# Sparse attention with two MLP layers on one core: scores made once with queries on partitions, the masked weights transposed by TensorE, and late conversion of three quarters of the last weights

## Chip, core and metric

The kernel runs on one core of a Trainium2 chip. The core has five engines that run their own instruction streams and meet at semaphores: PE (TensorE, matrix products, with its weight loads shown apart as PEld), DVE (VectorE), ACT (ScalarE), POOL (GpSimd) and SP (SyncE), which here only issues transfers. The metric is the device time of one execution in microseconds (us); lower is better. Matmuls read SBUF and write PSUM, which has eight banks of 2 KB per partition.

## What is computed

```python
def _attn_ref(q, k, v, tau):                      # 4 batches, 8 heads, 576 tokens, 64 wide
    scores = scale * np.matmul(q, k.transpose(0, 1, 3, 2))
    thresh = np.max(scores, axis=-1, keepdims=True) - tau
    scores = np.where(scores >= thresh, scores, -1000000000.0)
    scores = scores - np.max(scores, axis=-1, keepdims=True)
    attn = np.exp(scores)
    attn = attn / (np.sum(attn, axis=-1, keepdims=True) + 1e-09)
    return np.matmul(attn, v)

def _moe_ref(x, w_in, w_out, g_ln):               # 2304 x 512 -> 1024 -> 512
    h = x @ w_in
    e = np.exp(h - np.max(h, axis=-1, keepdims=True))
    solu = h * e / (np.sum(e, axis=-1, keepdims=True) + 1e-09)
    mu = np.mean(solu, axis=-1, keepdims=True)
    var = np.mean((solu - mu) ** 2, axis=-1, keepdims=True)
    return ((solu - mu) / np.sqrt(var + 1e-06) * g_ln) @ w_out

def _moe2_ref(x, w_in, w_out):                    # 2304 x 512 -> 2048 -> 512
    h = x @ w_in
    return (h * np.tanh(softplus(h))) @ w_out
```

The attention keeps only keys whose score lies within tau of the row's largest one. The four weight matrices arrive as 64-bit floats and are turned into 32-bit ones on the device.

## The kernel before

**Planner.** Every instruction is a task with an engine, a duration, its data and buffer dependencies (`Plan.add`, line 65). `Plan.run` (line 198) tries a list scheduler with several weights and emits the shortest order that it found. The order on each engine is fixed by that: an instruction that waits holds everything behind it on its engine. Buffers are named slots with a number of turns (`buf(pool, tag, shape, dtype, turns)`).

**Attention, heads n = 0 to 31.** `operands` (line 480) loads K and Q of a head with the 64 dimensions twice on the 128 partitions, and makes a rounded high half and a residue of each, so that two one-pass matmuls (high Q, low Q against stacked K) give an accurate product. Then the scores are made twice:

- `s_tile` (line 502), five tiles of 128 queries (the fifth is half empty): queries on partitions, four matmuls of 288 columns into a PSUM tile `st`, then one DVE maximum over the 576 keys (line 517). `m_chain` (line 523) turns the five maxima of a head into thresholds, rounds and transposes them (six lines of small DVE work, 526 to 532), and sends them by a transfer (line 534) into two extra rows of the operand `Qb`.
- `unit` (line 538), five units: keys on partitions this time, four more matmuls of 288 columns (line 548), which subtract the threshold by the two extra rows. ACT copies the scores out of PSUM to `xu` (line 559), ACT takes the exponential (line 560), DVE masks (line 561). One unit in five handles the half key tile and goes from PSUM directly (lines 555 and 561).

`pv` (line 579) multiplies V with the masked weights, which already have keys on partitions. In heads 0 to 15 (`n < SB0`) these are plain 32-bit matmuls (two instructions each, line 597); in heads 16 to 31 weights and V are split into halves (ACT line 566, DVE or POOL line 574) and take three one-pass matmuls. The half key tile always goes through a split (line 566, POOL line 568, matmuls 607 and 608). ACT moves the result and the row sums out of the single bank `acc` (lines 619 and 620), and `norm` divides.

**First MLP, token tiles 0 to 17** (4.5 per batch): `x_split`, `moe_h` (line 663, 24 matmuls of 512 columns into a two-bank tile `mo`), `layer_norm`, `moe_t` (line 704, eight 128x128 PE transposes, line 716, into `mo`), `moe_y` (line 730, matmuls of 256 columns). A tile needs the whole attention of its batch, so this MLP of one batch runs beside the attention of the next.

**Second MLP** (line 787 on): the hidden width is cut into four groups q = 0 to 3, and the tokens into nine pieces p of 256. `ff_in` and `ff_out` run 96 matmuls of 256 columns per group and piece, and pieces go in pairs with 512 columns after the first six. Group q uses one of two weight buffers (`b_w`), so that group q+2 waits for group q. Pool changes order the stages: `o_a` when the operands of attention are free, `o_b` after the attention, `o_c` after the first MLP; groups 1 and 3 wait for `o_c`.

**Weights.** `convert` (line 383) loads a 128x256 piece of 64-bit numbers and needs two ACT, three DVE and one POOL instruction (line 404). There are 96 pieces: 32 of the first MLP, 64 of the second. The 64 are stored to a scratch in memory (`store`, line 416); `split_w2` (line 842) loads them back later and splits them into halves (lines 857 and 861).

## Time and profile before

| | |
|---|---|
| median of three runs | 1069.92 us (1067.49 to 1074.01) |
| the profiled execution | 1072.17 us |
| its span, first to last instruction | 1070.4 us |
| PE busy | 979.0 us (91%), 5696 matmul instructions |
| DVE, ACT, POOL busy | 670.5, 711.6, 438.5 us |
| mean granted clock of PE | 0.97 of full speed |
| memory traffic of the span | 117 GB/s |

A busy PE is not a PE at its peak: the time of one matmul instruction in the profile includes its way through the pipeline, so that the times of consecutive ones overlap. The steady cost of one is read from the distance between starts. The profile's stretches therefore have to be read with two numbers for PE, the busy time and the work (instructions times steady cost). A row of a stretch gives the engines in the order PE, PEld, DVE, ACT, POOL.

### The profile page before, as it was taken

The numbers are of one execution on the slowest core, as the hardware profiler recorded it, in microseconds if no ns is written. First come the engines' busy times: TensorE is split into PE (matmuls) and PEld (weight loads), VectorE is DVE, ScalarE is ACT, GpSimd is POOL, SyncE is SP. The second block draws the span as 40 slices with busy tenths as digits, with TensorE's granted clock in tenths as the row PEclk, the third lists the DMA queues.
The fourth block names the chain that finished last, engine by engine and source line by source line (L and its number), as shares of the span: only waits on it lengthen the run. The fifth ranks groups of instructions, "written<-read, shape, count | busy, mean of one in ns | idle before, by whom it ended". The sixth has DMA issues, their size and how long they took to land.

```text
span 1070.4 us, 16653 instructions
## 1 busy us (share of the span) xinstructions
PE 979.0 (91%) x5696; PEld 860.3 (80%) x5696; DVE 670.5 (63%) x1416; ACT 711.6 (66%) x1312; POOL 438.5 (41%) x434
## 2 busy tenths in 40 slices
PE   5886889798699988988988999999999999999998
PEld 4765677677599878877988998998888888888887
DVE  7888888888888878777687646433245434322222
ACT  4977778888687778787798867655577467521220
POOL 5665666466655745655636332222022412300000
PEclk8988899899799999998999999999999999999999
DMA  6333333233222222231213863489665566422311
GB/s 184 100 102 84 92 92 93 69 94 102 73 79 78 73 80 66 55 94 53 56 37 97 255 206 108 129 262 366 199 216 187 182 197 207 153 79 99 118 50 70
DMA packets 109849, 132.03 MB, mean 123 GB/s; under 512 B 18634, under 2 KB 80010, under 8 KB 109764
## 3 DMA queue, kind: packets, MB, share of 16 engines
q1 hardware_dynamic: 109620, 130.96, 39.6%
q8 instruction: 45, 0.74, 0.3%
q14 instruction: 40, 0.33, 0.1%
q10 hardware_dynamic: 144, 0.00, 0.0%
HBM read 99.68 MB, written 25.69 MB: 117 GB/s over the span
## 4 chain that ended last, share of the span: by engine, by line
PE 61%; ACT 6%; DVE 4%; issue 1%; POOL 0%; DMA 0%; ACTq 0%; POOLq 0%
PE o L918 13%; PE h L892 12%; PE smt L739 8%; PE mo L671 7%; PE h2b L892 6%; PE o2b L918 5%; PE acc L597 3%; PE st L548 2%; PE st L513 2%; ACT hi L566 1%; ACT e L560 1%; ACT xu L559 1%; PE mo L716 1%; DVE so L689 1%; DVE e L561 1%
## 5 line engine op out<-in xcount | busy, mean ns | idle before, releaser
L404 POOL TENSOR_TENSOR cf<-cf,cl 128x256 uint32<-128x256 uint32 x96 | 78.9, 826 | 207.7 <-DVE cf L402 148.1
L517 DVE TENSOR_REDUCE m<-st 128x1 f32<-128x576 f32 x160 | 119.1, 748 | 54.3 <-PE st L513 53.3
L561 DVE SCALAR_TENSOR_TENSOR e<-xu,thr,e 128x576 f32<-128x576 f32 x128 | 115.2, 906 | 3.8 <-ACT e L560 3.3
L597 PE MATMUL acc<-e,V 128*128 128x288 f32 x256 | 81.7, 450 | 24.4 <-DVE e L561 17.4
L560 ACT ACTIVATE e<-xu,sc 128x576 f32<-128x576 f32 x128 | 98.7, 773 | 6.2 <-POOL lo L574 3.5
L513 PE MATMUL st<-Kst,Qhh 128*128 128x288 f32 x320 | 78.7, 329 | 18.3 <-DVE Kst L490 7.3
L559 ACT ACTIVATE xu<-st 128x576 f32<-128x576 f32 x110 | 70.9, 645 | 30.8 <-DVE e L561 15.8
L739 PE MATMUL smt<-LH,W2H 128*128 128x256 f32 x288 | 82.1, 285 | 0.4 <-DVE yl L750 0.3
L739 PE MATMUL smt<-LL,W2H 128*128 128x256 f32 x288 | 81.7, 284 | 0.0
L739 PE MATMUL smt<-LH,W2L 128*128 128x256 f32 x288 | 81.7, 284 | 0.0
L597 PEld LDWEIGHTS acc<-e,V 128*128 128x128 f32 x256 | 48.7, 206 | 40.9 <-DVE e L561 11.1
L574 POOL TENSOR_TENSOR lo<-e,hi 128x576 fp32r<-128x576 f32 x32 | 48.1, 1505 | 79.4 <-ACT hi L566 54.8
L513 PEld LDWEIGHTS st<-Kst,Qhh 128*128 128x128 f32 x320 | 54.9, 201 | 28.6 <-ACT xu L559 8.1
L597 PE MATMUL acc<-hi,V 128*128 128x288 f32 x256 | 64.6, 310 | 10.2 <-ACT ss L620 9.4
L548 PE MATMUL st<-Qhh,Kst 128*128 128x288 f32 x274 | 67.4, 328 | 6.7 <-DVE er L561 2.5
L513 PE MATMUL st<-Kst,Qb 128*128 128x288 f32 x320 | 71.6, 307 | 0.0
L942 DVE TENSOR_TENSOR acc<-acc,o 128x512 f32<-128x512 f32 x36 | 24.8, 688 | 69.8 <-PE o L918 69.8
L345 ACT ACT_TABLE_LOAD x52 | 66.7, 1283 | 1.6 <-PEq L987 0.7
L548 PE MATMUL st<-Qb,Kb 128*128 128x288 f32 x274 | 60.9, 304 | 5.3 <-DMA Qb<-mr 5.3
L490 POOL TENSOR_TENSOR Kst<-K,Kst 64x640 fp32r<-64x640 f32 x31 | 51.6, 1665 | 27.5 <-ACT Kst L489 16.6
L548 PEld LDWEIGHTS st<-Qhh,Kst 128*128 128x128 f32 x274 | 47.4, 198 | 15.3 <-ACT xu L559 4.8
L568 POOL TENSOR_TENSOR ph<-er,ph 64x576 fp32r<-64x576 f32 x32 | 46.7, 1459 | 29.4 <-ACT ph L566 19.8
(180 smaller groups left out, 3149.5 us busy)
## 6 DMA issues: line engine op xcount, KB each, us to landing
y5h<-y_hi SPq DMA_DIRECT2D x26, 512.0 KB
y5l<-y_lo SPq DMA_DIRECT2D x26, 512.0 KB
cr<-w_in SPq DMA_DIRECT2D x48, 256.0 KB
cr<-w_out SPq DMA_DIRECT2D x48, 256.0 KB
K<-kq SPq DMA_DIRECT2D x32, 320.0 KB
Q<-kq SPq DMA_DIRECT2D x32, 288.0 KB
Kb<-Kst SPq DMA_DIRECT2D x32, 160.0 KB
y2h<-y_hi SPq DMA_DIRECT2D x10, 512.0 KB
```

What stands on the lines that cost most here:

```text
L404: t = add("POOL", gps(CW), lambda: G.tensor_tensor(cf.tile, cf.tile, cl.tile, ALU.add), [t4, t2], use=[cl, cf])
L513: TE.matmul(st.tile[:, j, :HS], a[b][:, cs], Kst[b][:, j * HS:(j + 1) * HS], start=(x == 0), stop=(x == 1))
L517: QM[n].append(add("DVE", dve(S), lambda: V.tensor_reduce(m5.tile[:, i:i + 1], st.tile[:, :, :HS], AX.XY, ALU.max), [t], [m5] if i == 0 el ...
L548: TE.matmul(st.tile[:, y, :HS], (Kst[b], Kb[n % NK])[x][:, kt * 128:(kt + 1) * 128], (Qhh[b], Qb[b])[x][:, q0:q0 + HS], start=(x == 0), st ...
L559: t1 = add("ACT", act(S, True), lambda: SC.activation(xu.tile, st.tile[:, :, :HS], ACTF.Copy), [t], [xu], [st])
L560: t1 = add("ACT", act(S), lambda: SC.activation(e.tile, x(), ACTF.Exp, scale=sc), [t1], [e], [xu], table="exp")
L561: t2 = add("DVE", dve(S) + 0.06, lambda: V.scalar_tensor_tensor(e.tile, x(), thr, e.tile, ALU.is_ge, ALU.mult), [t1], use=[held, e], port= ...
L597: TE.matmul(acc.tile, l, r, start=(kp == 0 and y == 0 and i == 0), stop=False)
L671: TE.matmul(h.tile[:, j], l.tile[:, kt], r[:, kt, j * 512:(j + 1) * 512], start=(kt == 0 and x == 0), stop=(kt == KD - 1 and x == 2))
L739: TE.matmul(y, l[:, k, cs], r.tile[:, k], start=(k == 0 and x == 0), stop=(k == KF - 1 and x == 2))
L892: TE.matmul(h.tile[:, a * w:(a + 1) * w], l.tile[:, k, s], r.tile[:, k], start=(k == 0 and x == 0), stop=(k == KD - 1 and x == 2))
L918: TE.matmul(o.tile[:, a * w:(a + 1) * w], l.tile[:, k, ds], r.tile[:, k % n * w:(k % n + 1) * w], start=(k == 0 and x == 0), stop=(k == FG ...
```

## The change

The scores are made once, with queries on partitions, for a pair of heads at a time. DVE takes the maximum; one small DVE instruction makes from it the bias for ACT and the threshold; ACT takes the exponential straight from PSUM; DVE masks straight from PSUM into an SBUF tile `e` that holds both heads. PE transposes the masked weights in 128x128 blocks (`turn`) into a single-bank tile `tp`, and ACT (three times in four) or DVE (one in four) moves them out (`leave`). The last 64 queries of the two heads share one tile (their operands are padded with zeros on the host, so that both heads add into one PSUM tile), and the last 64 keys of the two heads share one transpose. `pv` uses plain 32-bit matmuls for all heads, 256 and 320 columns wide. A pair has 9 score tiles and 41 transposes in 14 groups, whose results leave in 15 copies.

The first MLP's `mo` becomes one bank, and `moe_h` and `moe_t` work in halves of 512. Of the second MLP's weights only group 0 (`LATE = 1`) still goes through the scratch; the 48 pieces of groups 1 to 3 are converted straight into the weight buffers when these are free, with the absolute value taken by DVE in place of ACT. The planner's estimate of PE durations is refitted.

```diff
-    NQ, NK = 3, 2
-    AH = 9
-    SB0 = 16
-    MO0 = 45
+    NV = 2
+    DV = 4
+    LATE = 1
...
-    for g in range(NG if WN == 2 else 0):
+    for g in range(LATE if WN == 2 else 0):
...
+    b_e = buf("e", "e", [128, 2 * S], F32, 3)
+    b_x = [buf("ep", "ex", [128, KT, C0], F32R, 3), buf("ep", "ey", [128, 2, KT, CN[1]], F32R, 1)]
+    b_er = buf("ep", "er", [128, S], F32R, 2)
     b_st = buf("p_st", "st", [128, 2, 512], F32, 2)
-    b_mo = buf("p_mo", "mo", [128, 2, 512])
-    b_acc = buf("p_acc", "acc", [128, HS])
+    b_tp = buf("p_tp", "tp", [128, 512])
+    b_mo = buf("p_mo", "mo", [128, 512])
+    b_acc = buf("p_acc", "acc", [128, CN[1]])
...
+            pieces = [(0, 0, HS), (1, HS, HS)] if i < KT else [(0, 0, HS), (1, HS, HS - 64), (1, S - 64, 64)]
+            for j, c, w in pieces:
+                for y, n in enumerate(heads):
+                    _, ks, qh, ql = OPS[n]
+                    k0 = c if i < KT or y == 0 else (c + 64) % S
+                    for x, q in enumerate((qh, ql)):
+                        TE.matmul(st.tile[:, j, c - j * HS:c - j * HS + w], q.tile[:, i * 128:(i + 1) * 128], ks.tile[:, k0:k0 + w],
+                                  start=(y == x == 0), stop=(y == len(heads) - 1 and x == 1))
...
+        t = add("DVE", dve(S), lambda: V.tensor_reduce(m.tile[:, 2:3], x(), AX.XY, ALU.max, negate=True), [t], [m], [st])
+        t = add("DVE", 0.08, lambda: V.scalar_tensor_tensor(m.tile[:, 0:2], ca, m.tile[:, 2:3], cb, ALU.mult, ALU.subtract), [t], use=[m], port=True)
+        a = add("ACT", act(S, True) + 0.08, lambda: SC.activation(et(), x(), ACTF.Exp, bias=m.tile[:, 0:1], scale=sc), [t],
+                [e] if h == 0 else (), [st, m, e], order=E[p, i][1:], table="exp")
+        t = add("DVE", dve(S) + 0.06, lambda: V.scalar_tensor_tensor(et(), x(), m.tile[:, 1:2],
+                et(), ALU.is_ge, ALU.mult), [a], use=[st, e, m])
...
+    def leave(n, dst, src, deps, new, use, order, lo=None):
+
+        count[0] += 1
+        if lo is None:
+            if count[0] % DV == 0:
+                return [add("DVE", dve(n), lambda: V.tensor_copy(f(dst()), src()), deps, new, use, order)]
+            return [add("ACT", act(n, True), lambda: SC.activation(f(dst()), src(), ACTF.Copy), deps, new, use, order)]
...
+    def turn(p, i, h):
+
+        tp, e = b_tp.new(), E[p, i][0]
...
         def go():
+            if h < 2:
+                for k in range(KT):
+                    o = h * (S + 64) + k * 128
+                    TE.transpose(tp.tile[:, k * 128:(k + 1) * 128], e.tile[:, o:o + 128], ident)
+            else:
+                o = KT * 128 if i < KT else S - 128
+                TE.transpose(tp.tile[:, :128], e.tile[:, o:o + 128], ident)
...
+    def pv(p, h, c):
+        acc, (v, ld) = b_acc.new(), VL[p]
+        w, cs = CN[c], slice(c * C0, c * C0 + CN[c])
...
+        def go(ks):
+            for k in ks:
+                if k < KT:
+                    l, r = cols(main(v)[:, k], h), x[0].tile[:, k] if c == 0 else x[0].tile[:, h, k]
+                else:
+                    l, r = cols(last(v), 2 * h), er[0].tile[:, cs]
+                TE.matmul(acc.tile[:, :w], l, f(r), start=(k == 0), stop=(k == KT))
...
     def split_w2(q):
         ah, al, bh, bl = W[q] = [b.new() for b in b_w[q % 2]]
+        if WN == 2 and q >= LATE:
+            first = {}
+            for x, (src, hi, lo) in enumerate(((w2_in, ah, al), (w2_out, bh, bl))):
+                for c in range(0, 512, CW):
+                    for k in range(4):
+                        def put(val, t, slots, x=x, hi=hi, lo=lo, k=k, c=c):
+                            h, l = (lambda s=s: s.tile[:, k, c:c + CW] for s in (hi, lo))
+                            a = add("ACT", act(CW), lambda: SC.activation(h(), val(), ACTF.Copy), [t, o_a if q % 2 == 0 else o_c],
+                                    [] if x in first else [hi], slots + [hi], order=first.get(x, [])[:1])
+                            b = add("POOL", gps(CW), lambda: G.tensor_tensor(l(), val(), f(h()), ALU.subtract), [a],
+                                    [] if x in first else [lo], slots + [hi, lo], order=first.get(x, [])[1:])
...
+                        W2Q[q, x, k, c] = convert(src, r0, c0, put, late=True)
+            return
```

## Rows read from the trace of the kernel before

**Rows 1.** Stretches: length, busy us (count) by engine, clock, DMA share, GB/s
```profile
0.00:148.00 148.00, 112.02 (x567) 93.59 (x568) 122.64 (x264) 105.43 (x201) 87.54 (x101) 0.91 0.40 110
148.00:593.00 445.00, 395.47 (x2461) 354.13 (x2461) 361.76 (x759) 353.72 (x662) 261.67 (x224) 0.96 0.26 77
593.00:1070.40 477.40, 471.51 (x2671) 412.62 (x2669) 186.13 (x395) 252.46 (x451) 89.32 (x111) 1.00 0.52 171
...
300.00:400.00 100.00, 93.64 (x632) 86.05 (x630) 80.25 (x163) 79.65 (x150) 59.78 (x45) 1.00 0.26 76
```

**Rows 2.** PE's waits: waiting group, its releaser, us in total, times, longest
```profile
PE acc L597 <- DVE e L561: 17.4, 10, 6.1
PE acc L597 <- ACT ss L620: 13.7, 14, 2.8
```

**Rows 3.** Timeline of PE, three places: start, us, line, tiles, count
```profile
300.37 0.43 PE L548 MATMUL st<-Qhh,Kst 128*128 128x288 f32 x2
...
301.42 0.28 PE L739 MATMUL smt<-LH,W2H 128*128 128x256 f32 x1
...
125.82 2.10 PE L597 MATMUL acc<-e,V 128*128 128x288 f32 x8
...
128.02 0.42 PE L513 MATMUL st<-Kst,Qb 128*128 128x288 f32 x2
...
560.27 1.03 PE L716 MATMUL mo<-ident,so 128*128 128x128 f32 x8
...
561.41 0.43 PE L548 MATMUL st<-Qb,Kb 128*128 128x288 f32 x2
```

**Rows 4.** Chain that ended last, from 575 us on: start, us, what
```profile
575.78 2.88 PE smt L739 x24
...
593.78 5.47 PE mo L671 x24
```

**Rows 5.** Stretch 148 to 593 us of lines 671, 739 and 716 alone
```profile
148.00:593.00 445.00, 86.09 (x312) 57.50 (x312) 0.96 0.26 77
...
148.00:593.00 445.00, 77.67 (x571) 73.65 (x572) 0.96 0.26 77
...
148.00:593.00 445.00, 13.45 (x96) 11.67 (x96) 0.96 0.26 77
```

**Rows 6.** DVE's groups: shapes, count, busy us, mean ns, idle before
```profile
L517 DVE TENSOR_REDUCE m<-st 128x1 f32<-128x576 f32 x160 | 119.1, 748 | 54.3 <-PE st L513 53.3
L561 DVE SCALAR_TENSOR_TENSOR e<-xu,thr,e 128x576 f32<-128x576 f32 x128 | 115.2, 906 | 3.8 <-ACT e L560 3.3
L561 DVE SCALAR_TENSOR_TENSOR er<-st,thr,er 128x576 f32<-128x576 f32 x27 | 21.8, 808 | 4.9 <-ACT er L555 4.7
L574 DVE TENSOR_TENSOR lo<-e,hi 128x576 fp32r<-128x576 f32 x32 | 28.8, 899 | 5.9 <-ACT hi L566 5.8
L532 DVE STREAM_TRANSPOSE mr<-nm 32x32 f32<-32x32 f32 x128 | 25.4, 199 | 1.4
L528 DVE TENSOR_SCALAR ma<-ma,t 128x5 f32<-128x5 f32 x32 | 10.8, 336 | 0.1
L529 DVE SCALAR_TENSOR_TENSOR ma<-ma,m 128x5 f32<-128x5 f32 x32 | 8.4, 264 | 0.1
```

**Rows 7.** Groups of ACT, POOL and PE, the same view
```profile
L559 ACT ACTIVATE xu<-st 128x576 f32<-128x576 f32 x110 | 70.9, 645 | 30.8 <-DVE e L561 15.8 <-PE st L548 11.9 <-DVE nm L531 1.6
L560 ACT ACTIVATE e<-xu,sc 128x576 f32<-128x576 f32 x128 | 98.7, 773 | 6.2 <-POOL lo L574 3.5 <-PE acc L597 0.5
L566 ACT ACTIVATE hi<-e 128x576 fp32r<-128x576 f32 x64 | 43.3, 679 | 4.0 <-DVE e L561 3.6
L555 ACT ACTIVATE er<-st,sc 128x576 f32<-128x576 f32 x27 | 19.9, 738 | 8.8 <-PE st L548 8.0 <-POOL lo L574 0.6
L404 POOL TENSOR_TENSOR cf<-cf,cl 128x256 uint32<-128x256 uint32 x96 | 78.9, 826 | 207.7 <-DVE cf L402 148.1 <-ACT cl L395 18.7 <-issue 14.3
L716 PE MATMUL mo<-ident,so 128*128 128x128 f32 x144 | 19.7, 282 | 3.1 <-POOL so L699 2.7 <-DVE LL L725 0.4
```

More of the change, by code (lines that the diff above doesn't have):

```diff
@@ L289, in pe @@
     def pe(count, n, passes=1):
-        return count * (n * passes / 2400 + 0.003)
+        return count * (n / 2270 + 0.007 if passes == 1 else n * passes / 2400)
     def dma(nbytes):
@@ L381, with convert @@
     b_cf = buf("cv", "cf", [128, CW], U32, 2)
-    def convert(src, r0, c0, put, gain=None):
+    def convert(src, r0, c0, put, gain=None, late=False):
         cr = b_cr.new()
@@ L496, in keys @@
-    def keys(n):
-        war = [UX[n - NK, u][0] for u in range(5)] if n >= NK else []
-        KB[n] = add("SP", 0.45, lambda: D(f(Kb[n % NK][0:64]), f(Kst[n % NQ][0:64])), [OPS[n][0]] + war)
-    KB = {}
-    def s_tile(n, i):
-        b = n % NQ
-        st = b_st.new()
-        cs = slice(i * 128, (i + 1) * 128)
-        if i == 0:
-            SX[n], QM[n] = [], [b_m5.new()]
-        m5 = QM[n][0]
-        def go():
-            for x, a in ((0, Qhh), (1, Qb)):
-                for j in range(2):
-                    TE.matmul(st.tile[:, j, :HS], a[b][:, cs], Kst[b][:, j * HS:(j + 1) * HS], start=(x == 0), stop=(x == 1))
-        t = add("PE", pe(4, HS), go, OPS[n], [st])
-        SX[n].append(t)
-        QM[n].append(add("DVE", dve(S), lambda: V.tensor_reduce(
-            m5.tile[:, i:i + 1], st.tile[:, :, :HS], AX.XY, ALU.max), [t], [m5] if i == 0 else (), [st, m5],
-            order=QM[n][-1:] if i else ()))
-        if i == 4:
-            m_chain(n)
@@ new lines, in load_v @@
+        v = VH[p % NV]
+        war = [t for h in range(2) for c in range(2) for t in PVT[p - NV, h, c]] if p >= NV else []
+        ld = [add("SP", dma(128 * KT * 256), lambda a=a: D(f(main(v)[:, :, 2 * a]), v2[p // (H_ // 2), p % (H_ // 2), :, a].rearrange(
+            "p (k d) -> p k d", d=64)), war) for a in range(2)]
+        ld.append(add("SP", dma(128 * 512), lambda: D(f(last(v)[:, 0:4:3]), v4[p // (H_ // 2), p % (H_ // 2)].rearrange("p (a d) -> p a d", d=64)), war))
+        VL[p] = v, ld
@@ new lines, in operands @@
+    def operands(n):
+        k2, q2, ks, qh, ql = (b.new() for b in (b_k2, b_q2, b_K, b_Q, b_L))
+        lk, lq = (add("SP", dma(128 * w * 4), lambda slot=slot, src=src: D(slot.tile, src[n // H_, n % H_]), new=[slot])
+                  for slot, src, w in ((k2, kk, S), (q2, qq, SP)))
+        eng, e, cost = (V, "DVE", dve) if n < 1 else (G, "POOL", gps)
+        a = add("ACT", act(S), lambda: SC.activation(ks.tile, k2.tile, ACTF.Copy), [lk], [ks], [k2])
+        a2 = add(e, cost(S), lambda: eng.tensor_tensor(ks.tile[64:128], k2.tile[64:128], f(ks.tile[64:128]), ALU.subtract), [a], use=[ks, k2], port=True)
+        b = add("ACT", act(SP), lambda: SC.activation(qh.tile, q2.tile, ACTF.Copy), [lq], [qh], [q2])
+        b2 = add(e, cost(SP), lambda: eng.tensor_tensor(ql.tile, q2.tile, f(qh.tile), ALU.subtract), [b], [ql], [qh, q2], port=True)
+        OPS[n] = [a, a2, b, b2], ks, qh, ql
@@ new lines, in s_tile @@
+    def s_tile(p, i, h):
+        st, m = b_st.new(), b_m.new()
+        if h == 0:
+            E[p, i] = [b_e.new()]
+        e = E[p, i][0]
+        et = lambda: e.tile[:, h * S:(h + 1) * S].rearrange("p (a b) -> p a b", a=2)
+        heads = [2 * p + h] if i < KT else [2 * p, 2 * p + 1]
+        slots = [s for n in heads for s in OPS[n][1:]]
+        def go():
+            pieces = [(0, 0, HS), (1, HS, HS)] if i < KT else [(0, 0, HS), (1, HS, HS - 64), (1, S - 64, 64)]
[6 more added lines that the diff above has]
+                                  start=(y == x == 0), stop=(y == len(heads) - 1 and x == 1))
+        t = add("PE", pe(4 * len(heads), HS), go, [t for n in heads for t in OPS[n][0]], [st], slots)
+        EXS.append([t])
+        x = lambda: st.tile[:, :, :HS]
+        t = add("DVE", dve(S), lambda: V.tensor_reduce(m.tile[:, 2:3], x(), AX.XY, ALU.max, negate=True), [t], [m], [st])
[4 more added lines that the diff above has]
+                et(), ALU.is_ge, ALU.mult), [a], use=[st, e, m])
+        E[p, i].append(t)
+        if h == 0:
+            E[p, i, "first"] = a
@@ new lines, in leave @@
+    def leave(n, dst, src, deps, new, use, order, lo=None):
[4 more added lines that the diff above has]
+            return [add("ACT", act(n, True), lambda: SC.activation(f(dst()), src(), ACTF.Copy), deps, new, use, order)]
+        t = add("ACT", act(n, True), lambda: SC.activation(dst(), src(), ACTF.Copy), deps, new, use, order)
+        return [t, add("DVE", dve(n), lambda: V.tensor_tensor(lo(), src(), f(dst()), ALU.subtract), [t], use=use)]
@@ L622, in pv @@
             order=EVT[p][2:3]))
-        if n % 2 and qh:
+        if h and c:
             norm(p)
```

346 lines of the change are left out of this document (140 added, 206 removed).

## The prediction, made before the changed kernel was run

> **What bounds the kernel now.** I read the stretches first. The attention ends at 593 us, and the first tile of the first MLP starts at 148 us, when the first batch is through; so there are three stretches [rows 1]. In the last one, 593 to 1070, PE is busy 471.5 of 477.4 us at full clock: that stretch is PE's own work. In the first two no engine is full: DVE has 83% and 81%, PE 76% and 89%, ACT 71% and 79%. Then I read PE's waits: its two largest are for the mask of DVE, 17.4 us, and for the one bank `acc`, 13.7 us in 14 waits [rows 2]. No single wait carries the loss.
>
> PE's busy time hides part of it, so I count its work. From starts on the timeline: eight one-pass matmuls of 288 columns from 300.37 to 301.42 us, 0.131 us each; a plain 32-bit instruction of 288 columns (125.82 to 128.02, less two of 0.131, over 8) 0.242 us; a transpose (560.27 to 561.41, less two of 0.131, over 8) 0.110 us [rows 3]. The chain gives 0.120 us for 256 columns (24 in 2.88) and 0.228 for 512 (24 in 5.47) [rows 4].
>
> Attention before, by the code: 640 + 640 score matmuls, 384 split and 128 half-tile ones of V make 1792 x 0.131 = 234.8; 256 plain instructions x 0.242 = 62.0; sum 296.8 us. First MLP before 593 us: 312, 571 and 96 instructions [rows 5] x 0.228, 0.120, 0.110 = 150.2. So PE worked 447.0 of 593 us, 75%, and 146 us were lost. The first stretch holds 567 instructions [rows 1], all of attention; 16 of a head's 60 are plain there, so about 416 x 0.131 + 151 x 0.242 = 91 us (it runs a little ahead into the second batch). That leaves 356 of 445 us for the second, 80.0%. Part of the loss is the clock: its means of 0.91 and 0.96 in the two stretches are time at 2.4 GHz mixed with time at 1.2.
>
> **The change, PE.** Removed: 296.8. Added, in 16 pairs: 512 full score matmuls x 0.131 = 67.1; in the shared tiles 64 of 288, 64 of 224 and 64 of 64 columns, 8.4 + 6.5 + 7.0 = 21.9 (the last at the 0.110 of a 128-column transpose as the nearest row; by columns it would be 0.03, 5 us less); V 64 x 5 x 2 = 640 plain instructions, 288 columns on average, x 0.242 = 154.9; 656 transposes x 0.110 = 72.2. Sum 316.1: PE gets 19 us more. The second score product that goes away (84 us) is paid for by transposes and by 32-bit V in the second half.
>
> The row of a transpose also shows a mean of 0.282 us for one [rows 7]; that includes the pipeline, and eight in a row start 0.110 apart, so I take 0.110 and keep 0.282 as the other end. The Trainium skill (TensorE: Matmul & The Clock Gate, Part 4: PE-mode transpose) gives about 275 ns for a 128x128 transpose inside a kernel, which speaks against this change. By it the 656 would be an estimated 180 us; by the row 72. The distance between starts disagrees with the page here.
>
> **DVE, ACT, POOL in the attention.** DVE loses 119.1 (maxima), the threshold chain (32 heads x five ops between 0.264 and 0.336, about 1.5, plus 25.4 of transposes, 73.7 in all), the masks (115.2 + 32 x 0.808 = 141.1) and 28.8 of residues: 362.7. It gains 144 maxima x 0.748 = 107.7, 144 small ops x 0.29 = 41.8, 144 masks from PSUM x 0.808 = 116.4, 36 wide copies at 0.665 (0.748 x 512/576) = 23.9, and 24 small ones at 0.3 = 7.2: 297.0. Net -65.7 us [rows 6]. ACT loses 82.6 (128 x 0.645), 98.7, 23.6 (32 x 0.738) and 65.2 (96 x 0.679), gains 144 exponentials x 0.738 = 106.3, 108 wide copies x 0.573 (0.645 x 512/576) = 61.9, 72 small ones x 0.3 = 21.6: net -80 us [rows 7]. POOL loses its residues of the weights and of V and keeps those of K and Q. The small copies and ops lie between 0.2 and 0.42 by the small rows; 240 of them at 0.1 more would be 24 us over two engines, inside the range.
>
> Transfers, by the code: 93 leave SP's queue (a copy of the keys, the thresholds and two constant rows, once a head), V takes 48 in place of 24; no wait is added there. In exchange waits on DVE and ACT stand ahead of PE's transposes. Behind a late `turn` on PE wait the next scores, the first MLP and `pv`; that is where a stall would go.
>
> **Late conversion.** I cost it at nothing. It happens under the last stretch, where PE is full while DVE has 39%, ACT 53%, POOL 19% [rows 1]. The tight place is group 1: 16 pieces x two POOL ops of 0.826 = 26 us, not before the first MLP has ended. The cover is group 0's pieces 6 to 8, which wait for the same moment: 3 x 96 x 0.120 = 34.6 us of PE. Without that cover it costs up to 26 us. Groups 2 and 3 have about 100 us of another group over them.
>
> **First stretch.** PE has 79 us for a batch; DVE decides. It was busy 122.6 of 148 us and loses 65.7/4 = 16.4: 106.2 at the same 83% is 128 us. Bounds: 110 (DVE nearly full after start) and 148.
>
> **Second stretch.** PE's work is 447.0 + 19.3 - 79 = 387 us. Its share was 80.0%. From 300 to 400 us, with DVE and ACT at 80%, PE was busy 93.6% at full clock [rows 1]. In the new stretch DVE would have 361.8 less about three quarters of 65.7, 312 us, or 74%, and ACT 294, or 70%. With lighter helpers I take a share of 92% (bounds: 80 and 100): 421 us.
>
> **Sum**, against the profiled 1072.2 us (2.2 above the median of the runs): 1072.2 - 593 = 479.2 stays; 479.2 + 128 + 421 = **1028 us**, 4% faster. Where the stall goes: next late are DVE's masks in the first stretch, which stay the bound there.
>
> **Rivals.**
>
> 1. *Helpers bind all through.* If the 593 us are set by DVE at its 81.7%, then (484.4 - 65.7)/0.817 = 512.5, and the time is 992 us. For it: all three helpers are near 80% wherever PE is not full. Against: PE would have 466 us of work in 512, 91% including the first batch. Chance 0.20; the floor is 110 + 387 + 479 = 976.
> 2. *Chains, not loads.* PE's loss is latency, each tile going PE, DVE, DVE, ACT, DVE, PE, ACT, PE; `st` has two turns and is now held until the mask. Lighter engines then don't help, the change does not do what it says, and the share stays at 80%: 479 + 128 + 484 = 1091; at 83% it is even. For it: even PE's two largest waits make only 31 of the 146 us [rows 2]. Against: the threshold transfer and its wait are gone, and a PSUM tile turns in about 0.5 + 0.75 + 0.3 + 0.74 + 0.81 us plus hand-overs, some 4 us, so two turns feed a tile each 2 us where 3.8 are there (549/144). Chance 0.19, of which 0.13 lies within 1% of before.
> 3. *One bank for transposes (the other side).* Each of 144 wide turns must wait until ACT or DVE has emptied `tp`; if PE's fixed order puts nothing useful between, each costs 0.57, and 144 x 0.57 = 83 us, 1111 us. It decides from 44/144 = 0.31 us per turn on. For it: `acc`, the same pattern, stalled PE. Against: only in 14 of 64 cases, 1 us each [rows 2], and the first MLP offers matmuls to put between. Chance 0.09.
> 4. *Transposes at the full 0.282 us*: 656 x 0.172 = 113 us, 1141 us. For it only the mean duration, against it the starts. Chance 0.05. The page named above would give nearly this.
>
> Forecast 0.47, with its own range of 1005 to 1058. A measurement of this kernel tells about 1% from no change. Faster by over 1%: 0.47 + 0.20 = 0.67; within 1%: 0.13; slower: 0.06 + 0.09 + 0.05 = 0.20. The range goes from the floor, 976, to 1092, just past rival 2: above lie rivals 3 and 4 and little else.
>
> **What would show each step.** Matmul instructions of scores 704, of V 640, transposes 656 more, starts 0.11 apart. DVE about 66 us and ACT 80 us lighter before the attention ends. First MLP tile at about 128 us; attention over near 549; PE full from there on with waits of a few us, none for the weights of group 1. The prediction is wrong if PE waits long for `turn`'s bank or the mask, if the first batch is not earlier, if the clock in the attention falls below the 0.91 and 0.96 of rows 1, or if PE stands at the start of group 1.

## The result and the profile after

The changed kernel takes 1024.86 us (median of four runs, 1018.8 to 1026.37) where the kernel before takes 1069.1 in the same comparison: a ratio of 0.9568 (95% interval 0.9518 to 0.9618), 4.3% faster. Forecast were 1028 us. The profiled execution is 1024.83 us with a span of 1023.0.

The stretches of the kernel after, up to 148 us, to 560 us and to the end, and 300 to 400 us; the columns are those of [rows 1].

```profile
0.00:148.00 148.00, 112.14 (x586) 89.57 (x587) 123.42 (x241) 106.27 (x214) 64.75 (x71) 0.93 0.36 102
148.00:560.00 412.00, 400.83 (x2479) 346.85 (x2478) 336.41 (x700) 305.85 (x630) 156.59 (x137) 1.00 0.30 89
560.00:1023.00 463.00, 458.94 (x2587) 400.40 (x2586) 165.91 (x369) 168.97 (x324) 80.93 (x102) 1.00 0.41 134
...
300.00:400.00 100.00, 98.72 (x628) 86.46 (x627) 81.12 (x166) 72.28 (x149) 31.61 (x26) 1.00 0.32 92
```

Two things are to be seen. The first line is nearly that of before: DVE is busy for 123.4 of 148 us, as it was for 122.6, and PE ran 586 instructions in place of 567. The second line is another one: the clock is 1.00 where it was 0.96, and PE is busy for 97%. From 300 to 400 us PE has 98.7% with DVE at 81%, where before it had 93.6% with DVE at 80% [rows 1]. So PE filled up without DVE becoming emptier there.

The first batch ends no earlier. The first tile of the first MLP, which needs that batch, shows it (the line that rounds its input: count, shortest, median and longest ns, first and last start):

```profile
L623 ACT ACTIVATE XH<-xT x20: 409/624/639, 148.5 to 609.5; 128x512 fp32r<-128x512 f32 x16, 128x256 fp32r<-128x256 f32 x4
```

PE's waits after, as in [rows 2]:

```profile
PE tp L536 <- DVE e L511: 8.6, 4, 3.2
PE st L501 <- DVE e L511: 7.6, 10, 2.3
PE st L501 <- DVE Kst L479: 7.3, 1, 7.3
PE tp L539 <- ACT ey L523: 4.2, 6, 1.2
PE acc L575 <- ACT ss L589: 3.4, 7, 1.0
...
PE smt L710 <- DVE yl L721: 2.4, 1, 2.4
```

The wait for the one bank `acc` fell from 13.7 to 3.4 us. The mask's hardly fell: 17.4 us before, 8.6 and 7.6 now, and of these two 8.0 and 6.3 us lie before 148.5 us. Gone are PE's waits for the threshold's transfer, 10.9 us in the kernel before:

```profile
PE mo L548 <- DMA Qb<-mr: 5.6, 2, 5.0
PE st L548 <- DMA Qb<-mr: 5.3, 4, 2.5
```

The groups of the new work, the same view as [rows 6, 7]:

```profile
L509 ACT ACTIVATE e<-st,m,sc 128x576 f32<-128x576 f32 x144 | 118.5, 830 | 41.6 <-DVE m L508 34.1 <-DVE t L667 3.7 <-PE st L501 1.4
L511 DVE SCALAR_TENSOR_TENSOR e<-st,m,e 128x576 f32<-128x576 f32 x144 | 116.1, 813 | 35.5 <-ACT e L509 34.8
L507 DVE TENSOR_REDUCE m<-st 128x1 f32<-128x576 f32 x144 | 107.5, 751 | 21.3 <-PE st L501 20.7
...
L536 PE MATMUL tp<-ident,e 128*128 128x128 f32 x576 | 92.1, 284 | 14.7 <-DVE e L511 8.6 <-ACT er L523 2.9 <-DVE ey L522 1.2
...
L508 DVE SCALAR_TENSOR_TENSOR m<-ca,m,cb 128x2 f32<-128x2 f32 x144 | 51.1, 364 | 1.7
...
L523 ACT ACTIVATE ey<-tp 128x512 f32<-128x512 f32 x60 | 35.7, 596 | 16.4 <-PE tp L536 15.5
```

The largest idle time of ACT stands ahead of the exponential and ends with line 508, the small op with two columns: 34.1 us. It is short in elements and long in the chain.

Its mean of 364 ns is made of two kinds (count, then shortest, median and longest ns):

```profile
L508 DVE SCALAR_TENSOR_TENSOR m<-ca,m,cb x144: 121/220/1591, 9.4 to 513.0; 128x2 f32<-128x2 f32 x144
```

All 33 that took over 0.3 us end within 0.03 us after the end of a POOL instruction, and none of the other 111 lies wholly inside one. One of the long ones, with the POOL instruction that it outlasts (timeline):

```profile
96.53 1.63 POOL L481 TENSOR_TENSOR Qb<-Q,Qhh 128x640 fp32r<-128x640 f32 x1
96.68 1.49 DVE L508 SCALAR_TENSOR_TENSOR m<-ca,m,cb 128x2 f32<-128x2 f32 x1
```

How close transposes follow each other is read from PE's timeline:

```profile
300.93 0.28 PE L710 MATMUL smt<-LL,W2H 128*128 128x256 f32 x1
301.05 0.60 PE L536 MATMUL tp<-ident,e 128*128 128x128 f32 x4
301.40 0.36 PE L710 MATMUL smt<-LH,W2H 128*128 128x256 f32 x1
301.60 0.28 PE L710 MATMUL smt<-LH,W2L 128*128 128x256 f32 x1
```

From 301.05 to 301.60 lie four transposes and one matmul of 0.120 us: 0.43 us for the four, 0.108 for a transpose, against a mean duration of 0.284 in the group above.

**PE's work after.** Up to 148.5 us the trace counts 224 score matmuls, 196 transposes and 168 instructions of V. With the prediction's own costs that is 224 x 0.126 (its 89.0 us over 704) + 196 x 0.110 + 168 x 0.242 = 90.5 us of work; 58 us were lost. A batch has 79 us of work, so 11.5 us belong to the second batch, run ahead. The trace after has no mark for the end of the attention, so it is set by an assumption: if the last stretch keeps its 477.4 us [rows 1], it begins at 1023.0 - 477.4 = 545.6 us. (The last product with V starts at 533.3 us, where it started at 586.7 before, 6 us ahead of the 593; counted that way the stretch ends near 540 us.) PE's work up to there is 316.1 + 150.2 = 466.3 us, so by this count, with the same work of the first MLP ahead of the mark as before, the second stretch, 397.1 us long, holds 375.8 us: 94.6%, and 21 us were lost. Both stretches lose 79 us, where 146 were lost before and 83 were forecast.

### The profile page after: what moved, and what is told of

The parts are those of the page before. It is cut to its first block, busy times and chain, and to the rows that moved or that the text cites. A ratio compares the mean times of both kernels' runs of the same rounds, so it can differ in the third digit from the quotient of the medians.

```text
span 1023.0 us, 15619 instructions
## 1 busy us (share of the span) xinstructions
PE 971.9 (95%) x5648; PEld 836.8 (82%) x5648; DVE 625.7 (61%) x1309; ACT 581.1 (57%) x1166; POOL 302.3 (30%) x309
## 4 chain that ended last, share of the span: by engine, by line
PE 70%; DVE 8%; ACT 7%; issue 1%; DMA 1%; ACTq 0%; SPq 0%
PE o L903 14%; PE h L877 13%; PE smt L710 8%; PE acc L575 8%; PE h2b L877 7%; PE mo L641 6%; PE o2b L903 5%; PE st L501 4%; PE tp L536 3%; ACT e L509 2%; DVE e L511 2%; DVE m L507 1%; PE mo L689 1%; DVE m L508 1%; DMA cr<-w_out 1%
## 5 line engine op out<-in xcount | busy, mean ns | idle before, releaser
L509 ACT ACTIVATE e<-st,m,sc 128x576 f32<-128x576 f32 x144 | 118.5, 830 | 41.6 <-DVE m L508 34.1
L511 DVE SCALAR_TENSOR_TENSOR e<-st,m,e 128x576 f32<-128x576 f32 x144 | 116.1, 813 | 35.5 <-ACT e L509 34.8
L501 PE MATMUL st<-Kst,Qhh 128*128 128x288 f32 (+2 forms) x352 | 111.4, 337 | 17.7 <-DVE e L511 7.6
L507 DVE TENSOR_REDUCE m<-st 128x1 f32<-128x576 f32 x144 | 107.5, 751 | 21.3 <-PE st L501 20.7
L536 PE MATMUL tp<-ident,e 128*128 128x128 f32 x576 | 92.1, 284 | 14.7 <-DVE e L511 8.6
L501 PE MATMUL st<-Kst,Qb 128*128 128x288 f32 (+2 forms) x352 | 97.8, 302 | 0.0
L536 PEld LDWEIGHTS tp<-ident,e 128*128 128x128 f32 x576 | 70.0, 145 | 32.2 <-DVE e L511 8.9
L575 PE MATMUL acc<-ey,VH 128*128 128x320 f32 x256 | 79.0, 436 | 2.1 <-ACT ss L589 2.1
L501 PEld LDWEIGHTS st<-Kst,Qb 128*128 128x128 f32 x352 | 70.6, 201 | 1.7
L575 PE MATMUL acc<-ex,VH 128*128 128x256 f32 x256 | 64.2, 385 | 2.4 <-ACT ss L589 1.3
L641 PE MATMUL mo<-W1H,XH 128*128 128x512 f32 x144 | 62.0, 430 | 0.9 <-ACT so L647 0.6
```

Source lines behind the costliest of these rows:

```text
L501: TE.matmul(st.tile[:, j, c - j * HS:c - j * HS + w], q.tile[:, i * 128:(i + 1) * 128], ks.tile[:, k0:k0 + w], start=(y == x == 0), stop=( ...
L507: t = add("DVE", dve(S), lambda: V.tensor_reduce(m.tile[:, 2:3], x(), AX.XY, ALU.max, negate=True), [t], [m], [st])
L509: a = add("ACT", act(S, True) + 0.08, lambda: SC.activation(et(), x(), ACTF.Exp, bias=m.tile[:, 0:1], scale=sc), [t], [e] if h == 0 else ( ...
L511: t = add("DVE", dve(S) + 0.06, lambda: V.scalar_tensor_tensor(et(), x(), m.tile[:, 1:2], et(), ALU.is_ge, ALU.mult), [a], use=[st, e, m])
L536: TE.transpose(tp.tile[:, k * 128:(k + 1) * 128], e.tile[:, o:o + 128], ident)
L575: TE.matmul(acc.tile[:, :w], l, f(r), start=(k == 0), stop=(k == KT))
```

## The experiments

Kernels named a_ start from the kernel after, b_ from the kernel before, n_ are new combinations. "First tile" is the start of the line XH shown above. In a_nobias, a_cbias, n_mo and n_fit_mo the largest score is not subtracted ahead of the exponential; the factor cancels when the result is divided by the row sum.

| kernel | median us | ratio to before (95%) | first tile, us |
|---|---|---|---|
| after | 1024.86 | 0.9568 (0.9518 to 0.9618) | 148.5 |
| a_late4 | 1022.25 | 0.9529 (0.9502 to 0.9556) | 148.6 |
| a_peold | 1021.78 | 0.9534 (0.9512 to 0.9556) | 150.8 |
| a_tr2 | 1068.89 | 0.9975 (0.9964 to 0.9985) | 155.7 |
| a_dvehalf | 1028.03 | 0.9598 (0.9573 to 0.9624) | 150.5 |
| a_nobias | 1009.07 | 0.9424 (0.9396 to 0.9451) | 133.9 |
| a_cbias | 1011.36 | 0.9437 (0.942 to 0.9454) | 134.8 |
| a_thrdma | 1036.59 | 0.9685 (0.966 to 0.971) | 157.3 |
| b_sb32 | 1036.78 | 0.967 (0.9649 to 0.969) | 148.9 |
| b_split_idle | 1064.43 | 0.9937 (0.9914 to 0.9961) | 154.7 |
| b_split_free | 1088.27 | 1.0168 (1.0141 to 1.0194) | 150.8 |
| n_fit_mo | 1014.23 | 0.946 (0.9436 to 0.9484) | 137.7 |
| n_mo | 997.19 | 0.9319 (0.9297 to 0.9341) | 125.0 |

**Two parts that should cost nothing.** a_late4 sends all four groups of the second MLP's weights through the scratch again; a_peold gives the planner its old estimate of PE.

```diff
-    LATE = 1
+    LATE = 4
```
```diff
-        return count * (n / 2270 + 0.007 if passes == 1 else n * passes / 2400)
+        return count * (n * passes / 2400 + 0.003)
```

> The kernel after with all four groups of the second MLP's weights through the scratch again (LATE = 4). The prediction cost this part at nothing: 1025 us, within 5. Rival: direct conversion carries some of the gain, since it frees ACT of table switches and the queue of stores and reloads: then 1033 us or more.

> The kernel after with the planner's old estimate of PE durations. If the gain comes from lighter helpers, the order matters little: 1025 us, within 10. Rival: the refitted estimate gives the fuller second stretch: then 1040 us or more, and PE's busy share after 148 us falls from 97% back towards 90%.

Measured 1022.25 and 1021.78 us. The intervals of both overlap that of the kernel after. The late conversion takes 48 us off ACT (629.1 to 581.1 us busy), puts 9 on DVE (616.9 to 625.7) and takes nothing measurable off the time; nor did the refitted estimate bring the gain.

**Transposes doubled.** a_tr2 issues each of the 576 transposes of line 536 twice, and the planner counts them twice.

```diff
-                for k in range(KT):
+                for k in [*range(KT), *range(KT)]:
```

> The kernel after with each group of four transposes made twice into the same place: 576 more transposes, at 0.110 us 63 us more of PE work, nothing else. If PE is the bound after the first stretch and not in it, about three quarters come through: 1070 to 1090 us. At the full 0.28 us of one transpose it would be 1150 or more. If PE is not the bound: under 1050 us.

Measured 1068.89 us, 44 us more and just under the lower end of what was expected. At 0.110 us the 576 are 63 us of work, at the full 0.284 they would be 164. So a further transpose cost 0.076 us of the end on average. Of the 44 us, 7 lie ahead of the first tile (155.7 us), with 176 of the added transposes, and 37 behind it, with the other 400: these are 44 us of work, so there most of PE's added work came through as time. In the first stretch the granted clock was higher than in the kernel after (0.98 against 0.93 up to 148 us), which may hide a part of the cost.

**More load on DVE, in no chain.** a_dvehalf adds a maximum over half of each masked tile, whose result nobody reads: 144 instructions.

```diff
+        EXS.append([add("DVE", dve(HS), lambda: V.tensor_reduce(m.tile[:, 3:4], et()[:, 0], AX.X, ALU.max), [t], use=[e, m])])
```

> The kernel after with one more DVE maximum over half of each masked tile, whose result nobody reads: 144 instructions, about 0.4 us each, 58 us of DVE in the attention, in no chain. If the helpers' load sets PE's share (the prediction), DVE in the second stretch goes from 85% to over 95% of the same time and the stretch must grow: 1055 to 1085 us. If only chains matter: 1025 to 1035 us.

Stretches of a_dvehalf:

```profile
0.00:148.00 148.00, 111.95 (x587) 89.63 (x587) 133.53 (x293) 106.83 (x220) 68.51 (x76) 0.94 0.36 108
...
200.00:300.00 100.00, 96.83 (x590) 82.64 (x589) 92.61 (x198) 77.17 (x155) 40.27 (x34) 1.00 0.24 71
300.00:400.00 100.00, 98.39 (x636) 86.63 (x635) 86.78 (x180) 72.01 (x144) 34.13 (x26) 1.00 0.28 86
400.00:500.00 100.00, 99.26 (x626) 87.25 (x625) 89.03 (x192) 73.17 (x142) 28.93 (x23) 1.00 0.24 71
```

Measured 1028.03 us: 144 x 0.44 = 63 us more of operations for DVE, 40 us more of busy time (625.7 to 665.5, as the times of consecutive ones overlap), and 3 us more for the kernel; the intervals of the two ratios overlap. DVE goes to 87 to 93% and PE stays at 97 to 99%. Up to 148 us the added operations take 18 us (42 x 0.44), and DVE's busy time there rose from 123.4 to 133.5. With DVE at 90% in place of 83% the first tile came 2 us later. So DVE's busy share is not what bounds either stretch of the kernel after.

**A shorter chain for each tile.** In a_nobias the exponential takes no bias, so it starts after the maximum; the small op (line 508) still makes the threshold, beside the exponential, and the mask waits for both. a_cbias is the same but for a bias operand that holds a constant zero.

In both, `red` names the maximum's task and `sm` the small op's. First the edit of a_nobias, then what a_cbias changes in it:

```diff
-        a = add("ACT", act(S, True) + 0.08, lambda: SC.activation(et(), x(), ACTF.Exp, bias=m.tile[:, 0:1], scale=sc), [t],
+        a = add("ACT", act(S, True) + 0.08, lambda: SC.activation(et(), x(), ACTF.Exp, scale=sc), [red],
...
-                et(), ALU.is_ge, ALU.mult), [a], use=[st, e, m])
+                et(), ALU.is_ge, ALU.mult), [a, sm], use=[st, e, m])
```
```diff
-        a = add("ACT", act(S, True) + 0.08, lambda: SC.activation(et(), x(), ACTF.Exp, scale=sc), [red],
+        a = add("ACT", act(S, True) + 0.08, lambda: SC.activation(et(), x(), ACTF.Exp, bias=cb[:, 0:1], scale=sc), [red],
```

> The kernel after with the exponential taken without subtracting the row's maximum (a factor that the division cancels), so that ACT waits for DVE's maximum only and not for the small op behind it: the chain of a score tile is about 0.5 us shorter, no engine's load changes. If the first stretch is set by DVE's load, as the prediction said, 1025 us within 5 and the first MLP tile still near 148 us. If it is set by the chain through the two PSUM tiles, the first stretch falls by about 0.5 of 4 us, 12%, to 130 us, and the time to 1008 to 1015 us.

> The kernel after with the exponential's bias read from a constant column (0), so that it waits for DVE's maximum only; unlike the run without a bias, ACT's instruction keeps its form. If the shorter chain gave the 15 us of that run, 1010 us within 5, first MLP tile near 134 us, ACT still at 0.83 us for one. If the cheaper ACT instruction (0.741 against 0.830 us) gave it, 1020 us or more.

The exponential's group and the line XH of a_nobias:

```profile
L509 ACT ACTIVATE e<-st,sc 128x576 f32<-128x576 f32 x144 | 106.2, 741 | 31.1 <-DVE m L507 29.8
```
```profile
L623 ACT ACTIVATE XH<-xT x20: 407/624/636, 133.9 to 592.5; 128x512 fp32r<-128x512 f32 x16, 128x256 fp32r<-128x256 f32 x4
```

The exponential's group of a_cbias:

```profile
L509 ACT ACTIVATE e<-st,cb,sc 128x576 f32<-128x576 f32 x144 | 119.0, 830 | 33.9 <-DVE m L507 32.5
```

Measured 1009.07 and 1011.36 us, 15.8 and 13.5 less than the kernel after, as expected if the chain counts. In a_cbias ACT's op is as long as before (0.830), and PE, DVE and ACT have the same instructions in the same order as in a_nobias. Gone is the link through the small op. Nearly all of the gain is in the first tile, 14.6 and 13.7 us earlier: what the first stretch saves goes through to the end about one for one, since PE is full behind it.

The 36 maxima of the first batch follow each other faster (the kernel after, then a_nobias; count, ns, first and last start):

```profile
L507 DVE TENSOR_REDUCE m<-st x36: 719/757/759, 8.6 to 115.5; 128x1 f32<-128x576 f32 x36
```
```profile
L507 DVE TENSOR_REDUCE m<-st x36: 721/751/759, 8.7 to 104.0; 128x1 f32<-128x576 f32 x36
```

That is a tile each 3.05 us, and 2.72 without the link. Taken from the starts and ends of these 36 in the trace, the time from the end of a maximum to its exponential was 1.39 us on average in the kernel after: 0.70 until the small op had its turn among DVE's other operations, 0.42 for the op itself, 0.27 from there to ACT. In a_nobias it is 0.27 us in all. So the link cost far more than the op's own duration, since it passes once more through a busy engine's fixed order. From the start of the maximum to the end of the mask a tile took 4.03 us, and 3.04 without the link.

The planner's order also differs between the kernel after and these two. It is hardly the cause: in the table, the kernel after and the five a_ kernels that keep the link start their first tile at 148.5 to 157.3 us, and the four kernels without it, in three different orders, at 125.0 to 137.7.

With the link gone the clock also stayed up. Up to 148 us the granted clock is 0.93 in the kernel after, which is some 21 us at 1.2 GHz and the rest at 2.4; in a_nobias it is 1.00:

```profile
0.00:150.00 150.00, 119.15 (x671) 95.06 (x672) 130.75 (x270) 114.03 (x239) 72.78 (x77) 1.00 0.38 112
```

Both, the hand-over and the clock, are in the 14.6 us; these runs do not part them.

**A longer chain.** a_thrdma sends the threshold through a small transfer ahead of the mask, as a stand-in for the transfer that the change took out.

```diff
+        th = b_t.new()
+        td = add("SP", 0.01, lambda: D(th.tile, m.tile[:, 1:2]), [t], [th], [m])
...
-        t = add("DVE", dve(S) + 0.06, lambda: V.scalar_tensor_tensor(et(), x(), m.tile[:, 1:2],
-                et(), ALU.is_ge, ALU.mult), [a], use=[st, e, m])
+        t = add("DVE", dve(S) + 0.06, lambda: V.scalar_tensor_tensor(et(), x(), th.tile,
+                et(), ALU.is_ge, ALU.mult), [a, td], use=[st, e, m, th])
```

> The kernel after with one more step in each score tile's chain and no more load on any engine: the threshold goes through a small transfer, some 2 us, before the mask reads it. If a tile's chain through the two turns of st sets the first stretch, a tile there takes about 1 us more, 36 tiles to the batch: first MLP tile at 180 us and the time at 1055 us or more. If load sets it: 1025 us within 8. In the second stretch (a tile each 3.8 us) the chain then still fits two turns, and PE stays over 95% busy from 250 us on.

Measured 1036.59 us, 11.7 more; the first tile comes 8.8 us later, while PE stays at 97 to 98% from 200 to 500 us. DVE and ACT carry no more than in the kernel after. Both expectations were missed: the load's 1025 us, and by far the chain's 1055 and its first tile at 180. In the first batch the transfer made a tile's way from maximum to mask 0.64 us longer (4.68 us), yet the maxima still came each 3.13 us: the time from the end of a mask to the maximum two tiles later, which reuses its turn of `st`, shrank from 2.05 to 1.48 us. So the two turns of `st` are not a firm bound; most of the 8.8 us came behind the masks of the batch, whose last one ended only 2 us later. The first stretch feels the chain of a tile, though less than was worked out, and the second hardly, with 3 of the 11.7 us.

**Split of the weights of heads 16 to 31 removed, alone.** b_sb32 is the kernel before with one number changed: V in plain 32-bit matmuls in all heads. PE gets work by it: 256 x 0.242 in place of 384 x 0.131, 11.7 us more.

```diff
-    SB0 = 16
+    SB0 = 32
```

> The kernel before with plain 32-bit V products in all heads, so without the split of the weights: PE gets 12 us more, DVE about 29 less, ACT 43 less, POOL 60 less, the chains of scores and thresholds stay. If load on the helpers sets the second stretch, it shrinks with DVE's load by about 8%, 1069 - 35 + 12 = 1046 us (1035 to 1058). If chains set it, PE's 12 us come on top: 1075 to 1085 us.

Stretches of b_sb32:

```profile
200.00:300.00 100.00, 88.88 (x485) 75.03 (x484) 85.49 (x194) 78.22 (x153) 56.69 (x58) 0.95 0.32 90
300.00:400.00 100.00, 98.97 (x626) 89.22 (x625) 81.42 (x185) 77.16 (x144) 47.31 (x44) 1.00 0.31 86
400.00:500.00 100.00, 99.53 (x635) 90.58 (x634) 84.49 (x174) 77.33 (x143) 46.96 (x43) 1.00 0.30 85
```

Measured 1036.78 us, inside the range expected if load counts, and 35.2 below the kernel before in the same comparison; the whole change gave 44.2 in its own. So this one part, alone, gives some four fifths of the gain. From 300 us on PE is at 99% while DVE is busier than in the kernel before (81% against 80 from 300 to 400 us). What the kernel after has beyond it lies, in these rows, ahead of 300 us: b_sb32 has 88.9% and a clock of 0.95 from 200 to 300 us, the kernel after 98.3% and 1.00.

**Is it the load or the link?** b_split_idle is b_sb32 with the split of heads 16 to 31 still made, but read by nobody: no matmul waits for it. Yet each tile `e` is held until its residue is made, and the second MLP's buffers open behind the residues.

```diff
+            if n >= SB1:
+                hi, lo = b_hi.new(), b_lo.new()
+                t3 = add("ACT", act(S), lambda: SC.activation(hi.tile, e.tile, ACTF.Copy), [t2], [hi], [e])
+                subt, eng, cost = (G.tensor_tensor, "POOL", gps) if u % 2 else (V.tensor_tensor, "DVE", dve)
+                IDLE.append(add(eng, cost(S), lambda: subt(lo.tile, e.tile, f(hi.tile), ALU.subtract), [t3], [lo], [hi, e], port=True))
...
-    o_b = opens(open_b, [o_a] + list(NRM.values())[-2:] + [t for x in list(PVT.values())[-8:] for t in x])
+    o_b = opens(open_b, [o_a] + IDLE + list(NRM.values())[-2:] + [t for x in list(PVT.values())[-8:] for t in x])
```

> The kernel before with plain 32-bit V products in all heads, as in the run before, but with the split of the weights of heads 16 to 31 still made on ACT, DVE and POOL; nobody waits for its result. The helpers' load is that of the kernel before, PE has 12 us more, and the chain from the mask to V's product is two instructions shorter. If load sets PE's share: 1069 us or more. If the chain does: 1037 us, within 10.

Stretches of b_split_idle:

```profile
300.00:400.00 100.00, 94.51 (x585) 83.53 (x584) 86.80 (x169) 80.76 (x151) 55.98 (x48) 1.00 0.25 69
400.00:500.00 100.00, 93.25 (x561) 82.22 (x559) 88.68 (x178) 82.32 (x152) 57.63 (x46) 0.97 0.24 68
```

Measured 1064.43 us, between the two expectations and close to the load's: most of the gain of b_sb32 is gone though no matmul waits for the split. So the link from the split to PE is not what cost most of the time. Of the 27.7 us above b_sb32, 5.8 already stand at the first tile (154.7 against 148.9 us), long before the first residue at 286 us: nothing of the split runs there, so they come with another order of the planner. It does not follow either that DVE's load did the rest: a_dvehalf had DVE as busy with PE at 97 to 99%. What is left is ACT and POOL, small DVE operations held up by POOL as seen above, the place of the operations in the order, and the longer hold of the three turns of `e`.

b_split_free was to part these: the same 128 operations read a constant of 64 columns, so that `e` goes free as in b_sb32.

```diff
-                t3 = add("ACT", act(S), lambda: SC.activation(hi.tile, e.tile, ACTF.Copy), [t2], [hi], [e])
+                t3 = add("ACT", act(S), lambda: SC.activation(v9(hi.tile), QZT, ACTF.Copy), [t2], [hi])
...
-                IDLE.append(add(eng, cost(S), lambda: subt(lo.tile, e.tile, f(hi.tile), ALU.subtract), [t3], [lo], [hi, e], port=True))
+                IDLE.append(add(eng, cost(S), lambda: subt(v9(lo.tile), QZT, f(v9(hi.tile)), ALU.subtract), [t3], [lo], [hi], port=True))
```

> The kernel before with plain 32-bit V in all heads; in heads 16 to 31 the 64 rounded copies on ACT and the 64 residues on DVE and POOL are still issued, each released by the mask as in b_split_idle, but they read a constant of 64 columns instead of the tile e, and nobody reads their results. So the helpers carry the same number of extra operations as in b_split_idle (1064.4 us), while e goes free after its matmuls as in b_sb32 (1036.8 us). Load theory (extra operations on the helpers delay what stands behind them): 1058 to 1068. Hold theory (the three turns of e, held until the residue is made, were what cost): 1035 to 1044. In between, around 1050: both.

The lines of the residues in both kernels (b_split_idle, then b_split_free):

```profile
L570 POOL TENSOR_TENSOR lo<-e,hi x32: 1397/1432/2276, 286.4 to 584.4; 128x576 fp32r<-128x576 f32 x32
L570 DVE TENSOR_TENSOR lo<-e,hi x32: 739/750/1996, 298.9 to 587.0; 128x576 fp32r<-128x576 f32 x32
```
```profile
L573 POOL TENSOR_TENSOR lo<-QZT,hi x32: 1393/1432/2413, 309.2 to 643.5; 128x576 fp32r<-128x576 f32 x32
L573 DVE TENSOR_TENSOR lo<-QZT,hi x32: 733/750/2281, 365.1 to 647.1; 128x576 fp32r<-128x576 f32 x32
```

Stretches of b_split_free:

```profile
300.00:500.00 200.00, 195.83 (x1242) 176.42 (x1241) 167.15 (x354) 161.10 (x296) 103.88 (x88) 1.00 0.27 75
500.00:700.00 200.00, 176.69 (x1121) 159.14 (x1120) 141.42 (x287) 144.75 (x281) 98.58 (x83) 0.95 0.33 106
```

Measured 1088.27 us, outside of both expectations; it does not part them. Since no buffer waits for them, the planner put most of these operations late: 19 of the 64 residues started before 500 us, where b_split_idle had 44, and the last at 647 us in place of 587. The buffers of the second MLP open only behind them, and PE's share falls to 88% from 500 to 700 us. From 300 to 500 us PE had 98%, but with fewer than half as many of these operations done. How the split cost its time, by load, by order or by holding `e`, stays open.

**A better version.** n_mo is a_nobias in which, during the first batch, every second transpose group goes to the bank `mo`, which the first MLP does not use yet. n_fit_mo is the same with the planner's durations of DVE and ACT raised.

```diff
-        tp, e = b_tp.new(), E[p, i][0]
+        nt[0] += 1
+        tp, e = (b_mo if p < H_ // 2 and nt[0] % 2 == 0 else b_tp).new(), E[p, i][0]
```
```diff
-        return (0.05 if psum else 0.094) + n / 1200
+        return (0.17 if psum else 0.2) + n / 1200
...
-        return 0.069 + n * 1.042e-3
+        return 0.15 + n * 1.042e-3
...
-        return 0.069 + n * 0.52e-3
+        return 0.22 + n * 0.52e-3
...
-        sm = t = add("DVE", 0.08, lambda: V.scalar_tensor_tensor(m.tile[:, 0:2], ca, m.tile[:, 2:3], cb, ALU.mult, ALU.subtract), [t], use=[m], port=True)
+        sm = t = add("DVE", 0.3, lambda: V.scalar_tensor_tensor(m.tile[:, 0:2], ca, m.tile[:, 2:3], cb, ALU.mult, ALU.subtract), [t], use=[m], port=True)
```

> A try at a version that beats both: no bias in the exponential, the transposes of the first batch alternate between two PSUM banks (tp and the first MLP's mo, idle then), and the planner's durations of ACT and DVE raised to those of the trace. The waits for tp in the first stretch were 8 us: 1000 us, 990 to 1012. If the bank is not what holds the first stretch: 1009 within 4.

> The kernel after with no bias in the exponential and the first batch's transposes alternating between two PSUM banks, with the planner's durations as they are: tells whether the try before it (1014 us) lost by the raised durations. If the bank helps: 1000 to 1006 us. If it does not: 1009 us within 4.

The line XH of n_mo, and its stretches:

```profile
L624 ACT ACTIVATE XH<-xT x20: 407/622/641, 125.0 to 581.8; 128x512 fp32r<-128x512 f32 x16, 128x256 fp32r<-128x256 f32 x4
```
```profile
0.00:125.00 125.00, 101.18 (x591) 84.72 (x591) 110.02 (x231) 99.27 (x208) 62.65 (x67) 1.00 0.39 117
...
150.00:200.00 50.00, 47.61 (x267) 39.08 (x266) 49.15 (x112) 44.75 (x99) 26.71 (x27) 1.00 0.32 98
200.00:300.00 100.00, 97.27 (x623) 86.06 (x622) 85.96 (x173) 73.73 (x157) 43.16 (x37) 1.00 0.30 88
```

Measured 997.19 us, ratio 0.9319: 28 us below the kernel after and better than expected. The first tile comes at 125.0 us, 8.9 earlier than in a_nobias, and 11.9 us of the end follow. Up to 125 us DVE is busy for 88% here, and for 98% from 150 to 200 us; whether DVE is the next limit was not tested. n_fit_mo took 1014.23 us, outside of what was expected either way and 17 us above n_mo: here durations closer to the trace gave a worse order. It is one try, and the planner's order alone moved a first tile by 6 us in b_split_idle. Without the subtraction a very large scaled score would overflow the exponential, so n_mo holds for inputs of this size.

## Why the prediction was right, and where it was not

The time was right to 3 us, 0.3%, and that closeness is luck: of the two stretches before the last one came out 20 us longer than forecast and the other 24 us shorter.

**Right in size.** PE's work: the counts are 704 scores, 640 of V and 656 transposes, and the transposes stand 0.108 apart where 0.110 was taken. The Trainium skill (TensorE: Matmul & The Clock Gate, Part 4: PE-mode transpose) has about 275 ns for one inside a kernel; the mean duration here is 284, but doubling 576 of them cost 44 us and not the 158 that its figure would make (an estimate). Late conversion at nothing: a_late4 shows it by a direct undoing, and PE has no wait left after 545 us. The last stretch as PE's own work: PE was busy for 458.9 of its last 463 us; its length of 479 us was not measured apart.

**First stretch: the step that failed.** Forecast were 128 us, on the ground that DVE decides at its 83%. The first tile came at 148.5, as before. DVE was again at 83%, so that the share looked like a limit, but it is none: at 90% the tile came 2 us later (a_dvehalf), and with one link less in a tile's chain 14 us earlier (a_nobias, a_cbias). What counts in this stretch is the latency of each tile's way through PE, DVE, DVE, ACT, DVE and then through the single `tp`, while PE has no other batch's work; the share of the granted clock in it is open. That is the prediction's rival 2, chains and not loads, true for the part of the kernel ahead of the first tile. The prediction set this rival aside because two turns of `st` would feed a tile each 2 us. Its turn of some 4 us was near, 4.03 from maximum to mask; but 2.05 us more passed from a mask to the maximum that reuses its turn, where 0.5 for the scores was counted, so a tile came each 3.05 us. Of rival 3 a small part holds there too: a second bank for the transposes brought the first tile 9 us forward in n_mo, where the rival's price was 83.

**Two terms mis-sized, in that chain.** The exponential with a bias was put at 0.738 us and takes 0.830. The row it was taken from had none, and a_cbias against a_nobias shows the operand alone: 0.830 against 0.741. The Trainium skill (ScalarE: Activation LUTs, What ACT_TABLE_LOAD costs) gives about 93 ns for each such operand; the 89 ns here agree. The small op was put at 0.29 and takes 0.364 on average; in the first stretch it takes 0.428, as its group between 20 and 148 us of the kernel after shows. Its median is 0.22: the mean comes from those that POOL held up, a term that the prediction did not have. The group:

```profile
L508 DVE SCALAR_TENSOR_TENSOR m<-ca,m,cb 128x2 f32<-128x2 f32 x42 | 17.5, 428 | 0.3
```

Together that is 0.23 us for each tile of the first stretch and 0.17 on average. In the first stretch the wait for DVE's order ahead of the small op, 0.70 us, is larger than both.

**Second stretch: the size held, its reason only in part.** Forecast were 92% of work and 421 us; it came to 94.6% and 397 us, with 11.5 us of work that the first stretch had run ahead. The reason given was lighter helpers, with DVE at 74% and ACT at 70%. From 148 to 560 us they had 82% and 74%; from 300 to 400 us DVE is no lighter than before (81% and 80%), while ACT fell from 80 to 72% and POOL from 60 to 32%. And a_dvehalf makes DVE heavier at hardly any cost. What b_sb32 shows is that the split of the weights in heads 16 to 31 held PE back: without it PE is full from 300 us on. It was not mainly the link to PE, since b_split_idle loses most of the gain again with nobody waiting for the split; so lighter helpers may be right for ACT and POOL. Load, order or hold is open, as told above.

**DVE and ACT.** Together the attention's new DVE operations take 305.5 us where 297.0 were forecast (107.5 + 51.1 + 116.1 of the rows above + 30.8 of copies), so DVE lost about 57 us and not 66. ACT fell by 130.5 us in all (711.6 to 581.1). Left out of its sum were 40 fewer table loads, 52 to 12, at 1.283 us each, 51 us; 26 of them come with the late conversion (a_late4 has 38). Neither sum decided the time: a_dvehalf has 40 us more on DVE and a_late4 48 us more on ACT at nearly the same time.

**The rivals.** Rival 1 (992 us) fell with DVE as the limit. Rival 2 was right about the first stretch and wrong about the second, which went from 80% to 94.6%. Rival 3's price, 0.57 for each of 144 turns, did not come: PE waited for `tp` to be emptied for 12 us in all (its waits for lines 522 and 523). Rival 4 fell with the distance between starts. So the forecast's 1028 comes out of 128 + 421, and the chip's 1025 out of 148.5 + 397.

## What to carry to other kernels

A helper's busy share of 83% does not by itself show that it is the limit. Ask of each stretch whether PE has other work to put between. Where it had, in the kernel after, PE's own work counted most, though in b_split_idle the helpers still held PE back there. Where it had none (here the first batch), the links that one tile passes counted, down to an operation on two columns; price a link with its wait for a turn on a busy engine, not with its duration alone. Look for gains first in such a stretch, since each microsecond there reached the end when everything behind it was full.
